# Raw weight halves kept in SBUF for their sums; joint accumulators read by ScalarE and added on GpSimd

## The chip, the cores and the metric

The kernel runs on one core of one Trainium2 chip. The metric is the device time of an execution in microseconds. Before the change the median of three runs is 1705.85 us (1702.62 to 1706.51). The profiled execution took 1705.2 us.

## The reference

Retention attention over 8 x 8 heads, then two two-layer networks on its rows; inputs are drawn as numpy arrays, the weights in float64.

```python
scores = (1 / sqrt(64)) * q @ k.T                      # 8 x 8 heads, 576 x 64
ret = scores * where(i >= j, gamma[h] ** (i - j), 0)   # decay by head
x = (ret @ v) -> 4608 x 512
h = x @ w_in           # 512 x 2048
g = h * sigmoid(1.702 * h)
x = g @ w_out          # 2048 x 512
h = x @ w_in2          # 512 x 2048
g = h - tanh(h)
out = g @ w_out2       # 4608 x 512
```

## The kernel before

Every product runs as three TensorE passes over a high and a low part of each operand (`PASS`), so each f32 tile is split before its use: a copy of the high part on ScalarE, a subtraction for the low part on VectorE. The 4608 rows form 9 blocks of 512; the 2048 hidden columns form 16 tiles (`NF`). A step is one block and one such tile.

The weights come as 64-bit patterns, in 64 chunks of 128 x 512, and are decoded on VectorE and ScalarE in thirds of a chunk (`dec_piece`); a step calls for one to three thirds. Decoded w_out and second-layer weights go to DRAM (`wd`), to be read again in each block.

The attention of a row tile is worked off in `attn_visit` at every second step, until all are done; GpSimd scales its inputs (`at_scale`). Blocks 0 and 1 of the first layer come in a part before the main loop. The main loop takes steps 32 to 143: blocks 2 to 8, sixteen steps each. A step issues the 12 matmuls of the first layer (`mm_in`, L616), perhaps an attention visit, the activation (`act_a`: tanh on ScalarE L630, the product on VectorE L632), the split of a tile for the second product (`split_direct`, ScalarE L728, VectorE L729), stores, and until step 82 four `outs` pieces, the second product (`mm_out`, L812). Blocks 2, 3 and 4 feed that product straight from SBUF; the others store g (`gd`) and load it later (`gl`, L723).

Some matrix products of blocks are formed by Strassen-like sums, which need fewer multiplications and sums of weights and of activations. Blocks 6 and 8 (`SUMMED`) form the activations' sums: `sums` (L1233 to L1236), five stores `gs` for each pair of steps (`stores`, L1206). The weights' sums are formed in two generators that are advanced one piece in each step of the main loop from step 48 on:

- `w2_prep` loads raw halves of w_in2 that the decoding had stored in DRAM (`wr`), splits them, forms sums on GpSimd (L960) and stores them (`wq`).
- `t_prep`, behind it, does so for w_out: loads of raw halves, 32 subtractions on VectorE (L995), 16 splits (ScalarE L990, VectorE L991), 16 stores `wt` (L981).

Both use the two tiles `spare` (four places, `room`), taken from the tag "y" at step 48.

Behind the main loop stand 16 steps of the second network's plain kind (`mm_std`, L1046), then 32 units of the paired kind (`mm_part` L1059, `copied`, `added` L1339, `act_2` L646 to L655). Between them `outs` hands out units of a second product. Of these, units 80 to 135 are joint: seven stages (`STAGES`) of eight units, with four accumulators in PSUM (`mm_joint`, L753). At a stage's end `evac_joint` empties them. Where nothing is to be added, ScalarE copies the accumulator into an "o" tile (L783); where a sum kept in DRAM is to be added, it was loaded by `kept_load` (L770, four loads at once, two units before the end), and VectorE reads accumulator and kept tile at once (L786). The result is stored on ScalarE's own DMA queue by `copies_out` (L824).

SP issues nearly all other DMAs, in program order: a DMA that waits for a semaphore holds those behind it. `w_ahead` issues the weight pairs (`wos`, L272; joint L286) and `g_ahead` the `gl` loads, both ahead of use; `wq_load` (L1027, L1036) loads the prepared sums of w_in2. The order of instructions on each engine is that of the code, which the helpers write by step numbers.

Of the kernel before, what the change touches and what calls it, by code (L numbers as in the profile page):

```python
# [54 lines left out]
def kernel(  # L55
# [45 lines left out]
    w2_d = {}  # L101
# [5 lines left out]
    part = {}  # L107

# [32 lines left out]
    def dec_b(m, f, c):  # L141
        hi, _, e, z = half[m, f, c]
        nc.vector.scalar_tensor_tensor(
            out=e, in0=hi, scalar=-(2 ** 31), in1=e, op0=ALU.bitwise_and, op1=ALU.bitwise_or
        )
        del stg[m, f, c]
        o = z.bitcast(F32)
        nc.vector.tensor_tensor(out=o, in0=z.bitcast(F32), in1=e.bitcast(F32), op=ALU.mult)
        half[m, f, c] = o
        if (m, c) == (1, 0):  # L150
            part[m, f, c] = half.pop((m, f, c))
        if (m, c) == (0, 1):
            part["raw", f, c] = o
# [8 lines left out]
    def dec_c(m, f, c):  # L162
# [6 lines left out]
        elif m == 0 and f % 5 < 3:  # L169
            sv = wos_p.tile([P, 2, DM], F32R, tag=f"wos{f % 5}", name="ws")  # L170
# [8 lines left out]
    def dec_d(m, f, c):  # L179
# [12 lines left out]
        if (m, c) == (0, 1):  # L192
            wos[f] = sv

    def dec_store():
        while part:
# [5 lines left out]
            if (m, c) == (1, 0):  # L202
                w2_d[f] = dram.tile([P, BLK], F32, tag=f"w{m}{f}{c}", name="wr")
                nc.sync.dma_start(out=w2_d[f], in_=sv)
                continue
# [4 lines left out]
    PAIRED = [q + i * NF // 2 for q in range(NF // 2) for i in range(2)]  # L210
    chunks = [(m, f, c) for m in range(2) for c in range(2) for f in (PAIRED if (m, c) == (1, 0) else range(NF))]
# [221 lines left out]
    def bat_x(b):  # L433
# [3 lines left out]
        if b % BPB == 0:  # L437
            xh[j], xl[j] = (
                x_p.tile([P, KD, BLK], F32R, tag="y" if j == 2 else "x", name=n, bufs=2 if j == 2 else 4)
# [149 lines left out]
    def step_of(o):  # L589
        v, f = divmod(o, NF)  # L590
        return ORDER[v] * NF + f if v < NB else o
# [81 lines left out]
    gs = {}  # L673
    n_items = n_steps + NJ
# [26 lines left out]
    def g_load(x):  # L701
# [6 lines left out]
        if spot == 0:  # L708
            gl[x] = t_p.tile([P, BLK], F32, tag="gl", name="gl", bufs=2)
# [48 lines left out]
    def kept_load(k):  # L758
# [3 lines left out]
        if name is None or q != NF // 2 - 3:  # L762
            return
        for y in range(4):
            r, m = divmod(y, 2)
            if y < 2:
                t = second["pool"].tile([P, BLK], F32, tag="o", name="kept", bufs=3)
            else:
                t = turn("t")
            nc.sync.dma_start(out=t, in_=kept_d[name, r, m])  # L770
            kept_t[y] = t

    def evac_joint(k, y):
# [4 lines left out]
        if base is None:  # L778
            if y < 3:
                o = second["pool"].tile([P, BLK], F32, tag="o", name="o", bufs=3)  # L780
            else:
                o = p_p.tile([P, BLK], F32, tag="p", name="o")
            nc.scalar.activation(out=o, in_=acc[y], func=ACTF.Copy, scale=0.5)  # L783
# [10 lines left out]
        copies.append((dst, o))  # L794
        copies_out(1)
# [67 lines left out]
    def g_ahead(x):  # L863

        while second and n_g[0] <= min(x + (7 if joint_item(x) else 4), n_b[0] + 3 + joint_item(x), n_items - 1):
# [14 lines left out]
    def out_units():  # L880

        for k in range(n_steps):
            w_ahead(k)
            if joint(k):
                kept_load(k)
                for y in range(4):
                    if y % 2 == 0:
                        g_ahead(N1 + 2 * (k - N1) + y // 2)
                    mm_joint(k, y)
# [6 lines left out]
            for m in range(4):  # L896
                mm_out(o, m)
# [10 lines left out]
    raw = {}  # L908
# [12 lines left out]
    def w2_prep():  # L921

        h = slice(0, DM // 2), slice(DM // 2, DM)
        waiting = []

        def store():
            while waiting:
                n, sv = waiting.pop()
                nc.sync.dma_start(
                    out=wq_d[q][:, n * 2 * DM:(n + 1) * 2 * DM], in_=sv.rearrange("p a n -> p (a n)").bitcast(F32)  # L930
                )

        def halves_of(n, src):
            sv = room[seen["room"] % 4]
            seen["room"] += 1
            kv = sv.rearrange("p a (k c) -> p (a k) c", c=2 * P).rearrange("p k (a c) -> p k a c", a=2)
            src = src.rearrange("p (k c) -> p k c", k=KD)
            nc.scalar.activation(out=kv[:, :, 0], in_=src, func=ACTF.Copy)
            nc.vector.tensor_tensor(out=kv[:, :, 1], in0=src, in1=kv[:, :, 0].bitcast(F32), op=ALU.subtract)
            waiting.append((n, sv))  # L940

        def load(q):
            raw[q] = [t_p.tile([P, DM], F32, tag="gl", name="wr", bufs=2) for _ in range(2)]
            for i in range(2):
                nc.sync.dma_start(out=raw[q][i], in_=w2_d[q + i * NF // 2])

        for q in range(NF // 2):
            while n_dec[0] < 3 * (2 * NF + 2 * q + 3):
                yield
            load(q)  # L950
            yield
            wq_d[q] = dram.tile([P, 8 * DM], F32, tag=f"wq{q}", name="wq")
            lo, hi = raw.pop(q)
            halves_of(0, lo)
            yield
            store()
            halves_of(2, hi)
            yield
            store()
            sub = lambda o, a, b: nc.gpsimd.tensor_tensor(out=o, in0=a, in1=b, op=ALU.subtract)  # L960
# [523 lines left out]
```

## Time and profile before

| | |
|---|---|
| median of three runs | 1705.85 us |
| the profiled execution | 1705.2 us, its span 1703.4 us |
| TensorE busy | 1651.0 us, 97% |
| VectorE, ScalarE, GpSimd busy | 1228.3, 886.6, 110.6 us |
| DMA | 510.60 MB, mean 300 GB/s |

The span is the time from the first to the last instruction that the profiler saw. PE is TensorE's matmuls, DVE VectorE, ACT ScalarE, POOL GpSimd, SP the engine that issues DMAs. PEclk is the granted share of TensorE's clock. An arrow in a wait points to what ended it. A DMA share of 1.00 means that all 16 transfer engines are busy.

### The profile page before, as it was taken

Reading aid. Unit: us, or ns where it says so; the run is one execution under the profiler, and the core shown is the slowest. Engines: PE = TensorE matmul, PEld = TensorE weight load, DVE = VectorE, ACT = ScalarE, POOL = GpSimd, SP = SyncE. Lnnn points to the kernel's source line nnn. Section 1 sums busy time; section 2 is a strip of 40 time slices with the busy share of each in tenths; the row PEclk is TensorE's granted clock in tenths of the full one; section 3 lists DMA queues with packets and bytes.
Section 4 is the critical chain, followed back from the end, with each engine's and each line's share of the span. In section 5 each row is a group of like instructions: output and inputs, shape, how many; then the busy total and the mean of one; then the engine's idle time right before and its main releaser. Section 6 shows DMA issues by size and latency. Waiting matters only on the chain.

```text
span 1703.4 us, 25300 instructions
## 1 busy us (share of the span) xinstructions
PE 1651.0 (97%) x8874; PEld 1342.8 (79%) x8874; DVE 1228.3 (72%) x1958; ACT 886.6 (52%) x1633; POOL 110.6 (6%) x99
## 2 busy tenths in 40 slices
PE   7999999999999998899999998999999999999999
PEld 4787888887888787688778777778888888888887
DVE  6787887778877866567678887777876777766632
ACT  5443433434433232456677666656665676656632
POOL 2101001212123100000000000000000000000000
PEclk9999999999999999999999999999999999999999
DMA  9666679888899989998899988989899988989962
GB/s 274 180 211 228 226 262 326 285 293 324 310 351 337 363 316 362 325 340 281 296 347 313 342 292 312 342 286 359 307 328 346 316 303 312 320 304 311 360 212 87
DMA packets 195503, 510.60 MB, mean 300 GB/s; under 512 B 21808, under 2 KB 31152, under 8 KB 186416
## 3 DMA queue, kind: packets, MB, share of 16 engines
q1 hardware_dynamic: 182704, 486.88, 82.2%
q10 hardware_dynamic: 12672, 22.11, 3.5%
q8 instruction: 70, 1.15, 0.3%
q14 instruction: 57, 0.47, 0.1%
HBM read 361.05 MB, written 147.85 MB: 299 GB/s over the span
## 4 chain that ended last, share of the span: by engine, by line
PE 75%; DMA 12%; DVE 8%; ACT 2%; issue 2%; SPq 1%; ACTq 0%; DVEq 0%
PE acc L816 23%; PE h L616 14%; PE acc L812 12%; PE x L1059 8%; PE acc L753 5%; PE y L1059 4%; PE h L1046 2%; PE w L1059 2%; DMA gs<-spare 2%; DMA gs<-t 1%; DMA gl<-gs 1%; DMA wos<-wd 1%; PE pat L538 1%; DMA gl<-gd 1%; DVE t L632 1%
## 5 line engine op out<-in xcount | busy, mean ns | idle before, releaser
L616 PE MATMUL h<-xh,wi 128*128 128x512 f32 x1152 | 372.3, 394 | 6.6 <-DVE t L632 5.8
L816 PE MATMUL acc<-wos,g 128*128 128x512 f32 x1344 | 329.6, 390 | 4.0 <-DVE kept L786 3.9
L816 PEld LDWEIGHTS acc<-wos,g 128*128 128x128 f32 x1344 | 252.4, 188 | 57.4 <-DVE kept L786 4.4
L728 ACT ACTIVATE g<-gl 128x512 fp32r<-128x512 f32 x222 | 139.3, 628 | 268.1 <-PE acc L816 173.2
L616 PEld LDWEIGHTS h<-xh,wi 128*128 128x128 f32 x1152 | 217.3, 189 | 56.3 <-DVE t L632 7.1
L729 DVE TENSOR_TENSOR g<-gl,g 128x512 fp32r<-128x512 f32 x222 | 152.1, 686 | 147.0 <-ACT g L728 146.4
L616 PE MATMUL h<-xl,wi 128*128 128x512 f32 x576 | 225.4, 391 | 0.4 <-DVE xl L445 0.4
L1059 PE MATMUL x<-xo,wq 128*128 128x512 f32 x768 | 195.1, 389 | 1.3 <-DVE h L1339 1.3
L812 PE MATMUL acc<-g,wos 128*128 128x512 f32 x768 | 189.0, 396 | 6.2 <-DMA wos<-wd 5.9
L812 PEld LDWEIGHTS acc<-g,wos 128*128 128x128 f32 x768 | 144.4, 190 | 39.2 <-issue 7.5
L1059 PEld LDWEIGHTS x<-xo,wq 128*128 128x128 f32 x768 | 144.0, 188 | 32.0 <-DVE h L1339 2.1
L131 ACT ACTIVATE e<-e,ebias 128x512 int32<-128x512 int32 x64 | 46.4, 724 | 208.1 <-DVE e L129 202.8
L632 DVE SCALAR_TENSOR_TENSOR t<-t,h 128x512 f32<-128x512 f32 x144 | 97.6, 682 | 54.4 <-ACT t L630 54.2
L653 DVE SCALAR_TENSOR_TENSOR pl<-pl,sq 128x512 f32<-128x512 f32 x144 | 99.5, 691 | 39.6 <-ACT pl L650 37.4
L630 ACT ACTIVATE t<-h 128x512 f32<-128x512 f32 x144 | 83.4, 587 | 85.1 <-PE h L616 59.9
L616 PEld LDWEIGHTS h<-xl,wi 128*128 128x128 f32 x576 | 108.7, 189 | 22.9 <-DVE xl L445 1.1
L655 DVE COPY_PREDICATED t<-marks,pl 128x512 f32<-128x512 int32 x144 | 109.4, 760 | 14.8
L753 PE MATMUL acc<-g,wos 128*128 128x512 f32 x408 | 104.9, 396 | 12.5 <-issue 3.7
L650 ACT ACTIVATE pl<-sq,abias 128x512 f32<-128x512 f32 x144 | 104.3, 724 | 4.7
L651 ACT ACTIVATE marks<-sq,sbias 128x512 f32<-128x512 f32 x144 | 102.0, 708 | 0.0
L753 PEld LDWEIGHTS acc<-g,wos 128*128 128x128 f32 x408 | 77.2, 191 | 31.2 <-issue 13.0
L1059 PE MATMUL y<-xo,wq 128*128 128x512 f32 x384 | 99.3, 395 | 0.0
(129 smaller groups left out, 2301.1 us busy)
## 6 DMA issues: line engine op xcount, KB each, us to landing
wos<-wd SPq DMA_DIRECT2D x176, 512.0 KB, 5.6
gd<-t SPq DMA_DIRECT2D x208, 256.0 KB, 5.2
gl<-gd SPq DMA_DIRECT2D x202, 256.0 KB, 5.3
wq<-wq SPq DMA_DIRECT2D x32, 1024.0 KB, 7.4
at<-in_attn_dram SPq DMA_DIRECT2D x29, 1024.0 KB, 6.6
stg<-in_w_dram SPq DMA_DIRECT2D x48, 512.0 KB, 6.7
wq<-wq SPq DMA_DIRECT2D x32, 768.0 KB, 8.9
wd<-ws SPq DMA_DIRECT2D x32, 512.0 KB, 5.4
```

Source lines behind the costliest of these rows:

```text
L616: nc.tensor.matmul(h, lhsT=win[f][:, a, k], rhs=xs[b][:, k], start=(n == 0), stop=(n == 3 * KD - 1))
L632: nc.vector.scalar_tensor_tensor(out=t, in0=t, scalar=1.0, in1=h, op0=ALU.add, op1=ALU.mult)
L650: nc.scalar.activation(out=pl, in_=sq, func=ACTF.Square, bias=abias)
L651: nc.scalar.activation(out=small, in_=sq, func=ACTF.Relu, bias=sbias, scale=-1.0)
L653: nc.vector.scalar_tensor_tensor(out=pl, in0=pl, scalar=CB, in1=sq, op0=ALU.add, op1=ALU.mult)
L655: nc.vector.copy_predicated(out=t, mask=small.bitcast(I32), data=pl)
L728: nc.scalar.activation(out=g[:, 0], in_=t, func=ACTF.Copy)
L729: nc.vector.tensor_tensor(out=g[:, 1], in0=t, in1=g[:, 0].bitcast(F32), op=ALU.subtract)
L753: nc.tensor.matmul(acc[y], lhsT=wo[:, a, m * P:(m + 1) * P], rhs=g[:, b], start=fresh and q == 0 and n == 0, stop=q == NF // 2 - 1 and n = ...
L812: nc.tensor.matmul(acc[m], lhsT=wh[:, m // 2, a, m % 2 * P:(m % 2 + 1) * P], rhs=g[:, b], start=first, stop=last)
L816: nc.tensor.matmul(acc[m], lhsT=g[:, a, c], rhs=wo[:, b], start=first, stop=last)
L1059: nc.tensor.matmul(ps, lhsT=wq[q][t][:, o // 2, o % 2 * 2 + k, a], rhs=xo[i][k][:, b], start=first and n == 0, stop=n == 5, skip_group_che ...
```

## The change

Three things change, and the order of pieces with them.

1. Raw w_out and w_in2 halves are decoded straight into one of three places in SBUF (`raw_place`). They belong to `room`, which now has five places: four in the `spare` tiles and one in a "gl" tile; the other two take the splits' results. Only the first three pairs of w_out still go through DRAM (`AWAY`). A pair that is complete joins a list `todo`, and each step advances the list by one or two pieces. If a place is wanted while its pair is still in `todo`, the list is advanced there and then. The chunks of w_out and the steps of block 2 follow the order of pairs (`PAIRED`); decoding goes at three thirds a step up to step 50, two up to step 82 and slower behind it.
2. `evac_joint` always reads the accumulator by ScalarE; a kept tile is added on GpSimd. The result goes out in `stores`, on SP. Kept tiles are loaded one by one, one unit before the end, all in "t" tiles.
3. `w_ahead` is called behind the first quarter of a unit in place of ahead of it; stores of the activations' sums come in another order, and two of their tiles come from `room`.

```diff
@@ raw_place, dec_b @@
+    def raw_place():
+        i = turn_of["raw"] % 3
+        turn_of["raw"] += 1
+        while users.get(i) in todo:
+            some_todo(1)
+        users[i] = "open"
+        return room[i].bitcast(F32), i
...
-        o = z.bitcast(F32)
+        i, q = divmod(f, NF // 2)
+        if m == c or m == 0 and q < AWAY:
+            o = z.bitcast(F32)
+        else:
+            if i == 0:
+                pairs_raw[m, q] = raw_place()
+            o = pairs_raw[m, q][0][:, i]
         nc.vector.tensor_tensor(out=o, in0=z.bitcast(F32), in1=e.bitcast(F32), op=ALU.mult)
@@ dec_d @@
+            i, q = divmod(f, NF // 2)
+            if i and q < AWAY:
+                late_t.append(q)
+                late_start()
+            elif i:
+                t, n = pairs_raw.pop((m, q))
+                raw_to(t_prep(q, t), n)
@@ g_load @@
-            gl[x] = t_p.tile([P, BLK], F32, tag="gl", name="gl", bufs=2)
+            gl[x] = room[4][:, gl_turn[0] % 2].bitcast(F32)
@@ kept_load @@
-        if name is None or q != NF // 2 - 3:
+        if name is None or q != NF // 2 - 2:
             return
...
+        if y == 0:
+            stores(0)
+        kept_t[y] = t = turn("t")
+        nc.sync.dma_start(out=t, in_=kept_d[(name, *divmod(y, 2))])
@@ evac_joint @@
+        nc.scalar.activation(out=o, in_=acc[y], func=ACTF.Copy, scale=0.5)
+        if base is not None:
+            t, o = o, kept_t.pop(y)
+            nc.gpsimd.tensor_tensor(out=o, in0=t, in1=o, op=ALU.add)
...
-            o = kept_t.pop(y)
-            nc.vector.scalar_tensor_tensor(out=o, in0=acc[y], scalar=0.5, in1=o, op0=ALU.mult, op1=ALU.add)
...
-        copies.append((dst, o))
-        copies_out(1)
+        done.append((dst, o))
@@ out_units @@
-            w_ahead(k)
             if joint(k):
-                kept_load(k)
                 for y in range(4):
                     if y % 2 == 0:
                         g_ahead(N1 + 2 * (k - N1) + y // 2)
+                    if y == 1:
+                        w_ahead(k)
+                    kept_load(k, y)
                     mm_joint(k, y)
@@ main loop @@
-            dec_piece(2 if j == 2 or (j < 5 and n % 2) else 1)
-        some(prep, 1)
+            dec_piece(2 if n < 3 * NF + BEHIND else int(n < PAUSE or j == 7))
+        if n == 6 * NF - 1:
+            some_todo(999)
+        elif n < PAUSE:
+            some_todo(1 if n < 3 * NF + BEHIND or n % 2 else 2)
+        else:
+            some_todo(1)
```

How instructions move is shown at three places. First VectorE in block 2, in a step before (L632 and L729 are the activation and the split, the rest decodes a chunk):

```order
L632 SCALAR_TENSOR_TENSOR t<-t,h 128x512
L729 TENSOR_TENSOR g<-t,g 128x512
L143 SCALAR_TENSOR_TENSOR e<-stg,e 128x512
L148 TENSOR_TENSOR z<-z,e 128x512
L185 TENSOR_TENSOR ws<-z,ws 128x2x256
L129 TENSOR_SCALAR e<-stg 128x512
L132 TENSOR_SCALAR z<-stg 128x512
L503 TENSOR_TENSOR p<-pat,mt_sb 128x512 x2
L137 SCALAR_TENSOR_TENSOR z<-stg,z 128x512
```

The same stretch of a step after (L690 and L789 are the activation and the split; L1026 and L986 are t_prep's subtractions and its split):

```order
L690 SCALAR_TENSOR_TENSOR t<-t,h 128x512
L789 TENSOR_TENSOR g<-t,g 128x512
L190 SCALAR_TENSOR_TENSOR e<-stg,e 128x512
L1026 TENSOR_TENSOR spare<-spare 128x256 x4
L986 TENSOR_TENSOR room<-spare,room 128x2x256
L986 TENSOR_TENSOR spare<-spare 128x2x256
L201 TENSOR_TENSOR spare<-z,e 128x512
L241 TENSOR_TENSOR ws<-spare,ws 128x2x256
L176 TENSOR_SCALAR e<-stg 128x512
L179 TENSOR_SCALAR z<-stg 128x512
L1026 TENSOR_TENSOR spare<-spare 128x256 x2
L561 TENSOR_TENSOR p<-pat,mt_sb 128x512 x2
```

Eight instructions of t_prep, from the steps 107 to 130 before, stand in one step of block 2.

Second, the end of a joint stage. Before, VectorE (L649 to L655 are a second-layer unit's activation, `kept<-acc` and `t<-acc` the evacuation):

```order
L729 TENSOR_TENSOR wos<-gl,wos 128x512
L786 SCALAR_TENSOR_TENSOR kept<-acc_9132,kept 128x512
L786 SCALAR_TENSOR_TENSOR kept<-acc_9136,kept 128x512
L649 TENSOR_TENSOR t<-h_9352,t 128x512
L653 SCALAR_TENSOR_TENSOR pl<-pl,sq 128x512
L654 SCALAR_TENSOR_TENSOR pl<-pl,h_9352 128x512
L655 COPY_PREDICATED t<-marks,pl 128x512
L729 TENSOR_TENSOR wos<-gl,wos 128x512
L786 SCALAR_TENSOR_TENSOR t<-acc_9145,t 128x512
L786 SCALAR_TENSOR_TENSOR t<-acc_9149,t 128x512
```

After, ScalarE at a stage's end (L704 to L709 are its part of such a unit, L788 copies of a split, L1356 a copy):

```order
L788 ACTIVATE wos<-room 128x512
L838 ACTIVATE o<-acc_8990 128x512
L838 ACTIVATE o<-acc_8995 128x512
L704 ACTIVATE t<-h_9207 128x512
L706 ACTIVATE sq<-h_9207 128x512
L708 ACTIVATE pl<-sq,abias 128x512
L709 ACTIVATE marks<-sq,sbias 128x512
L1356 ACTIVATE m_9336<-y 128x512
L788 ACTIVATE wos<-gl 128x512
L838 ACTIVATE o<-acc_9003 128x512
L838 ACTIVATE o<-acc_9007 128x512
```

The two pairs of evacuations keep their distance from each other, with a unit's activation between them, on the other engine; GpSimd has twenty adds L841 behind its scaling of the attention's inputs.

Third, SP in block 8. Before, stores of w_out's sums (`wt`) stand among the activations' (`gs`), with loads `a` for the next sums:

```order
L981 DMA wt<-spare 128x1024 x2
L659 DMA gd<-t 128x512
L1206 DMA gs<-a_6264 128x512
L1206 DMA gs<-t 128x512
L1206 DMA gs<-spare 128x512
L1221 DMA a_6363<-gd 128x512 x2
L981 DMA wt<-spare 128x1024
L1206 DMA gs<-spare 128x512
L1206 DMA gs<-t 128x512
L981 DMA wt<-spare 128x1024
```

After, in block 8:

```order
L1230 DMA gs<-spare 128x512
L1230 DMA gs<-t 128x512
L1230 DMA gs<-spare 128x512
L1230 DMA gs<-t 128x512
L1230 DMA gs<-spare 128x512
L1245 DMA a_6411<-gd 128x512 x2
L1047 DMA wq<-wq 128x1024 x2
```

The wt stores are gone from these rows, and the first wq load stands behind a group of five stores.

## Rows read from the trace of the kernel before

**Rows 1.** The page's first part: busy time, share and count of each engine.
```profile
PE 1651.0 (97%) x8874; PEld 1342.8 (79%) x8874; DVE 1228.3 (72%) x1958; ACT 886.6 (52%) x1633; POOL 110.6 (6%) x99
```
**Rows 2.** TensorE's waits from 400 us on: total, times, longest.
```profile
PE acc L812 <- DMA wos<-wd: 5.9, 1, 5.9
PE h L616 <- DVE t L632: 5.8, 2, 4.2
PE acc L753 <- DVE t L786: 4.8, 4, 2.9
PE acc L816 <- DVE kept L786: 3.9, 1, 3.9
PE acc L753 <- issue: 3.7, 1, 3.7
PE acc L753 <- DMA wos<-wd: 3.4, 1, 3.4
PE acc L753 <- DVE kept L786: 2.1, 2, 1.2
```
**Rows 3.** Windows: length, busy time of PE, PEld, DVE, ACT, POOL, PEclk, DMA share, GB/s.
```profile
1180.00:1460.00 280.00, 280.00 (x1237) 231.86 (x1236) 212.43 (x318) 186.67 (x325) 0.00 (x0) 1.00 0.91 318
660.00:720.00 60.00, 48.97 (x192) 39.15 (x191) 32.08 (x50) 18.30 (x32) 0.00 (x0) 0.89 0.95 341
697.90:704.70 6.80, 6.13 (x15) 4.80 (x16) 3.16 (x5) 4.13 (x7) 0.00 (x0) 0.50 1.03 406
840.00:1120.00 280.00, 259.47 (x1108) 209.53 (x1107) 222.39 (x341) 186.76 (x325) 0.00 (x0) 0.98 0.91 320
162.33:273.26 110.93, 110.93 (x710) 90.02 (x708) 87.86 (x155) 45.33 (x87) 12.20 (x9) 1.00 0.75 256
```
**Rows 4.** ScalarE's waits from 640 to 690 us.
```profile
ACT t L630 <- DMA gs<-t: 17.5, 3, 7.7
```
**Rows 5.** DMA issues of the execution: count, size, median us to landing.
```profile
wr<-z SPq DMA_DIRECT2D x32, 256.0 KB, 5.1
wr<-wr SPq DMA_DIRECT2D x32, 256.0 KB, 5.8
wt<-spare SPq DMA_DIRECT2D x16, 512.0 KB, 5.2
wq<-wq SPq DMA_DIRECT2D x16, 512.0 KB, 7.2
```
**Rows 6.** Line 981: ns min/median/max, first and last start.
```profile
L981 SPq DMA_DIRECT2D wt<-spare x16: 319/413/1156, 577.3 to 644.2; - x16
```
**Rows 7.** Timeline of SP: start, us, instruction.
```profile
686.71 2.21 SPq L1027 DMA_DIRECT2D wq<-wq  x4
689.02 1.26 SPq L272 DMA_DIRECT2D wos<-wd  x2
```
**Rows 8.** Lines 786 and 783: count, busy us, mean ns, idle before.
```profile
L786 DVE SCALAR_TENSOR_TENSOR t<-acc,t 128x512 f32<-128x512 f32 x10 | 6.4, 682 | 0.0
L783 ACT ACTIVATE o<-acc 128x512 f32<-128x512 f32 x8 | 4.3, 589 | 0.0
```
**Rows 9.** Timeline of VectorE at the stage end near 990 us.
```profile
990.82 1.28 DVE L786 SCALAR_TENSOR_TENSOR t<-acc,t 128x512 f32<-128x512 f32 x2
```
**Rows 10.** Timeline of VectorE, line 137, in block 2.
```profile
211.74 1.81 DVE L137 SCALAR_TENSOR_TENSOR z<-stg,z 128x512 f32<-128x512 uint32 x1
...
218.72 0.68 DVE L137 SCALAR_TENSOR_TENSOR z<-stg,z 128x512 f32<-128x512 uint32 x1
```
**Rows 11.** Timeline of GpSimd in the same stretch.
```profile
211.69 1.30 POOL L332 TENSOR_TENSOR at<-at,qt_sb 128x512 f32<-128x512 f32 x1 [22.00 <-DMA at<-in_attn_dram]
```
**Rows 12.** Lines 995 and 991: t_prep's work on VectorE.
```profile
L995 DVE TENSOR_TENSOR wr<-wr 128x256 f32<-128x256 f32 x32 | 13.5, 421 | 0.6
L991 DVE TENSOR_TENSOR spare<-wr,spare 128x512 fp32r<-128x512 f32 x16 | 11.0, 686 | 5.3 <-ACT spare L990 5.3
```
**Rows 13.** VectorE's waits from 162.33 to 273.26 us.
```profile
DVE sbd L555 <- ACT xh L548: 9.8, 3, 3.3
```

More of the change, by code (lines that the diff above doesn't have):

```diff
@@ L107, with some, raw_to, some_todo @@
     part = {}
+    AWAY = 3
+    PAIRED = [q + i * NF // 2 for q in range(NF // 2) for i in range(2)]
+    room = []
+    todo = []
+    pairs_raw = {}
+    users = {}
+    turn_of = {"raw": 0, "sv": 0}
+    def some(it, n):
+        for _ in range(n):
+            next(it, None)
+    def raw_place():
[3 more added lines that the diff above has]
+            some_todo(1)
+        assert users.get(i) != "open"
+        users[i] = "open"
+        return room[i].bitcast(F32), i
+    def raw_to(it, i):
+        users[i] = it
+        todo.append(it)
+    def some_todo(n):
+        while n and todo:
+            try:
+                next(todo[0])
+                n -= 1
+            except StopIteration:
+                todo.pop(0)
+    late_t = []
+    def late_start():
+        while room and late_t:
+            q = late_t.pop(0)
+            t, n = raw_place()
+            for i in range(2):
+                nc.sync.dma_start(out=t[:, i], in_=r_d[q + i * NF // 2])
+            raw_to(t_prep(q, t), n)
+    def sv_place():
+        turn_of["sv"] += 1
+        return room[3 + turn_of["sv"] % 2]
     def wload(m, f, c):
@@ L756, in mm_joint, with kept_load @@
             )
-    def kept_load(k):
+    def kept_load(k, y):
         stage, q = divmod(k - N1, NF // 2)
         name = STAGES[stage][3]
-        if name is None or q != NF // 2 - 3:
+        if name is None or q != NF // 2 - 2:
             return
[L764 to L771, printed above, removed]
+        if y == 0:
+            stores(0)
+        kept_t[y] = t = turn("t")
+        nc.sync.dma_start(out=t, in_=kept_d[(name, *divmod(y, 2))])
     def evac_joint(k, y):
@@ L863, in g_ahead @@
     def g_ahead(x):
[L865 removed]
+        while second and n_g[0] <= min(x + (7 if joint_item(x) else 4), n_b[0] + 3 + joint_item(n_g[0]), n_items - 1):
             g_load(n_g[0])
@@ L933, in halves_of @@
[L933 to L960, printed above, removed]
-            sub(hi[:, h[0]], hi[:, h[0]], lo[:, h[0]])
-            sub(hi[:, h[1]], hi[:, h[1]], hi[:, h[0]])
-            sub(lo[:, h[0]], hi[:, h[1]], lo[:, h[0]])
-            sub(lo[:, h[1]], lo[:, h[1]], hi[:, h[1]])
-            yield
-            halves_of(1, hi)
-            yield
-            store()
-            halves_of(3, lo)
-            yield
-            store()
-            yield
@@ L1215, in firsts_load @@
         if u % 3 == 2:
-            ts = [t_p.tile([P, BLK], F32, tag="z", name="a1", bufs=3) for _ in range(2)]
+            ts = [room[3].bitcast(F32)[:, i] for i in range(2)]
         else:
@@ L1301 @@
             wq_load(0, True)
-    some(prep, 99)
     stores(1)
+    assert not todo and n_dec[0] >= 3 * (len(chunks) + 2), n_dec
     for q in (1, 2):
```

170 lines of the change are left out of this document (87 added, 83 removed).

## The prediction

> **What bounds the kernel now.** I read the busy times first. TensorE is busy for 1651.0 us, 97% of the span of 1703.4 us [rows 1], and the change leaves the number of its matmuls as it was. So three things can move the time: gaps in TensorE's work that close, gaps that open, and stretches at the lower of its two clocks. Next I read the waits of TensorE after 400 us [rows 2]. They name the second half's gaps: 5.8 us for the first layer's activation (L632), 5.9 us for a weight pair (wos), 10.8 us in all (4.8 + 3.9 + 2.1) for VectorE's evacuation of a joint accumulator (L786), and beside these 3.7 us of "issue" and 3.4 us for another weight pair. Last I read windows, to see what a gap costs with what follows it [rows 3]. From 1180 to 1460 us TensorE is never idle and does 1237 matmuls in 280 us, 4.42 in a microsecond, 0.226 us each. From 660 to 720 us 265 would go in and 192 did: 73 x 0.226 = 16.5 us are lost, though its busy share shows only 11. The rest is the clock: the 6.8 us right behind the gap for wos ran at 0.50 (1.2 of 2.4 GHz) and took 15 matmuls where 30 go, 3.4 us lost after the gap itself. From 840 to 1120 us, the joint units, 1108 matmuls ran: 129 x 0.226 = 29 us lost.
>
> From 162 to 273 us, block 2 (the first of the main loop), TensorE is busy for the whole 110.93 us [rows 3]. So the change can take from two places, and it puts new work into a third that is full.
>
> **The end of the first layer, 660 to 720 us.** What ends the wait for L632 is two steps away: ScalarE's tanh (L630) waited 17.5 us for stores gs<-t [rows 4], because it writes into a tile that a store still reads. Those stores are late because the transfer engines are full: a share of 0.95 at 341 GB/s [rows 3]. The change takes transfers out from right before this stretch. Before, each raw half of w_out and w_in2 is stored (wr<-z, 32 x 0.26 MB) and loaded again for its sums (wr<-wr, 32 x 0.26 MB, 16 of them w_out's), and w_out's sums are stored (wt<-spare, 16 x 0.52 MB) [rows 5], at 577 to 644 us [rows 6]. Those 16 loads and 16 stores are 12.6 MB, at 341 GB/s 37 us of full transfer engines, in the 85 us before the stretch. After, 26 of the 32 raw stores and 26 of the 32 loads are gone, and the stores wt stand in block 2's steps, where the share is 0.75 [rows 3]. With 37 us of transfers out of the way, stores that are late by 6 us should be in time: the gap of 5.8 us and some 3.4 us at half speed behind it go, with what is lost in shorter waits beside them 10 us. The second gap, for wos, has another cause: SP issues four loads wq right ahead of that pair [rows 7], 0.52 MB each [rows 5], 2.1 MB or 6 us at 341 GB/s, and these stay; two gl loads of 0.26 MB are even put ahead of it. So I take the first gap alone. Bounds: 0, if the last block's own stores fill the queue again, and 16.5, if all goes. I take -10.
>
> **The joint units, 840 to 1120 us.** The sums that are added to a kept one are read on VectorE, 20 instructions of 0.68 us, ten of them into a "t" tile; the stages without a kept sum are read by ScalarE, 8 instructions of 0.59 us [rows 8], and no wait in [rows 2] names L783. The 0.68 us are not the wait of up to 4 us. That is VectorE's queue: at the stage end near 990 us two L786 start at 990.82 us [rows 9], behind a second-layer unit's four instructions and a split in the same queue, and TensorE can't begin the next sum in that bank before. After, ScalarE reads every accumulator into a tile of its own, and GpSimd adds the kept tile behind it, off TensorE's path. ScalarE has a queue as well, but it is busy for 186.76 of the 280 us, VectorE for 222.39 [rows 3]. What is late next is ScalarE's own string of four activations of a second-layer unit and a split's copy, near 0.6 us each. A gap half as long as the one for wos is taken to cost half as much behind it, 1.7 us at half speed, and two of these gaps are of that size (2.9 and 3.9 us): 10.8 + 3.4 = 14 us, of which I take 12. The other 15 us of the stretch's loss are weight pairs, "issue" and gaps too short for a row: the kept loads now come one by one instead of four at once ahead of gl loads, and 28 stores leave ScalarE's queue for SP's. I give that -4, so -16 in all. Bounds: -8 (half of the L786 gaps come back as waits for ScalarE) and -21 (all 14, and the 7.1 of "issue" and wos).
>
> There are new costs here. GpSimd's 20 adds can hold VectorE; a kept tile sits in a "t" tile until GpSimd has added and SP has stored it; and SP stands at that store until GpSimd is done, with loads of weights queued behind it. In the trace of before a VectorE instruction (L137) took 0.68 us alone and 1.81 us while GpSimd worked [rows 10, 11]: 1.1 us a time, twenty times 22 us if each add held VectorE to that degree and all of it lay on the path; nothing if VectorE's 58 idle us of the 280 hide it. I take +3, near the lower end, because an evacuation no longer stands in VectorE's queue. The Trainium skill, "GPSIMD Engine Reference", section "8. Key points", says that GpSimd shares its SBUF interfaces with VectorE, and names contention with VectorE instructions that read two SBUF inputs. The trace agrees, with 1.81 us against 0.68 us; by that rule alone the adds would be dear in the joint units, where most of VectorE's work is of that kind, and the fourth rival is what it would give.
>
> **Block 2, 162 to 273 us.** Here w_out's sums go: 32 subtractions (13.5 us) and 16 splits (11.0 us) [rows 12], with 16 copies on ScalarE, which has room. VectorE is busy for 87.86 of 110.93 us [rows 3], so 23.07 us are free and 24.5 come: at least +1.4, if every idle moment is filled. It won't be. Of the idle time 9.8 us are the attention's waits for a copy on ScalarE [rows 13], long enough (3.3 us) for another instruction to stand in them; the rest is spread over short waits between two steps of one unit, and a queue in order can't use those for certain. Then 24.5 - 9.8 = +14.7 us. I take the middle, +8. It would show as TensorE waiting for a split (L729, line 789 after) or for L632 (line 690 after).
>
> **Sum.** 1705.2 - 10 - 16 + 3 + 8 = 1690 us for a run like the profiled one. That run (1705.2 us) stands 0.65 us under the median of 1705.85; I leave the sum as it is. The 26 raw stores that go from the early blocks I cost at nothing: the share there is 0.75 and TensorE has no gap.
>
> **Rivals.** First, all opens: the gap for wos goes too, since the queue is drained (-16.5), the joint units give -21 with no new cost, and VectorE fills every gap (+1.4): 1705.2 - 36.1 = 1669 us. For it: 37 us of transfers gone; against it: the 2.1 MB right ahead of wos.
> Second, the transfers were hidden anyway: the last block's own stores fill the queue and the first gap stays (0), the joint units give -12, and block 2 costs the full 14.7: 1708 us. For it: the last store wt is issued at 644 us [rows 6], and behind 660 us the share is still 0.95; against it: the joint units run at 320 GB/s without a gap of that length for a store.
> Third, slower: VectorE becomes the bound in block 2. Its queue is in order, so subtractions ahead of a split delay the unit that TensorE is about to take. If all 24.5 us come on the path, in four gaps of some 6 us, each followed by 3.4 us lost at half speed, that is 24.5 + 13.6 = 38 us, and with the other terms 1705.2 - 26 + 3 + 38 = 1720 us. It decides once TensorE loses more than 23 us between 162 and 275 us. For it: 24.5 us into 23.07; against it: TensorE has no wait there now, so the splits run ahead of it.
> Fourth, GpSimd holds VectorE in the joint units for the whole 22 us, on the path: 1705.2 - 10 - 16 + 8 + 22 = 1709 us.
> Fifth, the change doesn't do what it says: the places in SBUF come free too late, the sums stay late, nothing moves: 1705 us. The order of instructions speaks against it.
>
> **Chances.** The forecast 0.56, with 1676 to 1700 us as its own range (block 2 between 1.4 and 14.7, the other two places 6 us either way); the first rival 0.20, the second 0.09, the third 0.08, the fourth 0.05, the fifth 0.02. The range for 8 in 10 reaches from just under the first rival to just over the fourth, 1667 to 1711 us. A measurement of this kernel can tell 0.2%, 3.4 us, from no change. Faster by more than that: 0.56 + 0.20 and a fifth of the second, 0.78. Within it: half of the second, half of the fourth, the fifth, 0.09. Slower: the third and what is left of the second and fourth, 0.13.
>
> **What would show it.** In the joint units TensorE's waits should name no VectorE evacuation, and the reads by ScalarE (line 838 after) should cost under 3 us in all. The tanh's wait for gs<-t should be under 3 us, 660 to 720 us should hold some 235 matmuls, and a wait for wos of about 6 us should stay. Between 162 and 273 us VectorE should be busy for over 95% of the time, and TensorE should show some 7 us of waits for lines 789 or 690. The forecast is wrong if block 2's losses exceed 23 us, if the gap for L632's successor between 660 and 690 us stays, or if VectorE's instructions beside a GpSimd add take over 1.5 us.

## The result, and the profile after

The changed kernel takes 1726.66 us (1720.52 to 1729.16, four runs) against 1706.18 us: a ratio of 1.0118, interval 1.0086 to 1.015. It is slower by 20 us where 16 us less were forecast. The profiled execution has a span of 1727.3 us, 23.9 more than before.

TensorE does the same 8874 matmuls. It is busy for 10.7 us longer, for the most part because more of them run at the lower of its two clocks (1.2 of 2.4 GHz): the mean granted clock is 0.986, against 0.990 before, and 0.014 of the span less 0.010 of the span before is an estimated 7 us:

```profile
PE 1661.7 (96%) x8874; PEld 1347.4 (78%) x8874; DVE 1227.7 (71%) x1938; ACT 895.9 (52%) x1653; POOL 141.0 (8%) x119
```

Where the time went is read best from the start of the same matmul in both traces. The table has the difference (after less before, us) that each stretch adds; the numbers are worked out from the starts in the two traces.

| stretch, to the start of | before, us | added | forecast |
|---|---|---|---|
| block 2's first second-layer product | 166.7 | +0.4 | 0 |
| step 56 (block 2 and the steps behind it) | 301.4 | +10.8 | +8 |
| step 76 (steps 56 to 75) | 428.4 | +3.6 | 0 |
| step 132 (steps 76 to 131) | 641.1 | -1.9 | 0 |
| end of the first layer | 728.7 | -3.4 | -10 |
| first joint unit | 836.2 | 0.0 | 0 |
| joint units and the first units behind | 1129.2 | +14.4 | -13 |
| the rest | 1688.2 | +0.2 | 0 |

Only the joint units went the other way from what was forecast. TensorE's waits of the changed kernel from 400 us on (total, times, longest) answer to [rows 2]:

```profile
PE acc L813 <- DMA wos<-wt: 11.0, 5, 3.3
PE acc L813 <- DMA wos<-wd: 7.4, 2, 5.3
PE acc L866 <- DMA wos<-wd: 6.7, 1, 6.7
PE x L1079 <- DVE h L1361: 6.4, 3, 3.1
PE x L1079 <- ACT u L1356: 3.5, 1, 3.5
PE acc L866 <- DVE g L789: 3.0, 1, 3.0
```

The 10.8 us for the evacuation (L786) are gone, as forecast, and so is the 5.8 us gap for the first layer's activation. In their place the joint units wait 18.4 us for weight pairs and 9.9 us for parts of second-layer units (h, u), which earlier came in time. The windows answer to [rows 3], with the same columns: block 2, the end of the first layer, the joint units, and two stretches around the end of the first layer.

```profile
162.80:284.50 121.70, 115.41 (x712) 91.14 (x710) 110.58 (x203) 53.05 (x102) 11.94 (x9) 0.99 0.83 281
671.00:731.00 60.00, 50.28 (x207) 40.70 (x206) 33.32 (x51) 20.21 (x36) 0.00 (x0) 0.91 0.96 351
845.70:1145.00 299.30, 268.59 (x1130) 215.43 (x1129) 227.28 (x325) 198.47 (x350) 30.64 (x20) 0.97 0.88 308
600.00:640.00 40.00, 40.00 (x299) 32.38 (x299) 16.18 (x28) 10.21 (x21) 0.59 (x1) 1.00 0.36 136
680.00:720.00 40.00, 30.28 (x119) 24.15 (x118) 19.44 (x30) 12.97 (x22) 0.00 (x0) 0.87 1.01 379
```

In block 2 VectorE went from 87.86 to 110.58 us, 91% of a stretch that is 10.8 us longer (over 95% were forecast). At the end of the first layer 207 matmuls ran in 60 us, not the 235 forecast. In the joint units no engine is full, so the loss is in the order of waiting. ScalarE at the end of the last joint stage (start, us, instruction, idle before) shows it:

```profile
1129.88 1.08 ACT L838 ACTIVATE o<-acc 128x512 f32<-128x512 f32 x2
1136.17 0.60 ACT L704 ACTIVATE t<-x 128x512 f32<-128x512 f32 x1 [5.21 <-issue]
```

The reads of the accumulators (L838) are quick. Then the next tanh (L704) stands for 5.2 us. The profile names nothing that ended this wait ("issue"), but the tanh began 0.07 us after a kept sum's store had landed (1136.10 us). The tanh writes a "t" tile, and all second-layer results and the four kept sums of a stage take turns in six of these. Between 850 and 1145 us the tanh's waits for a t tile are these, first after, then before:

```profile
ACT t L704 <- DMA gd<-t: 12.4, 4, 4.6
ACT t L704 <- DMA x<-t: 7.4, 2, 6.5
ACT t L704 <- issue: 5.2, 1, 5.2
```
```profile
ACT t L646 <- DMA gd<-t: 7.5, 3, 4.6
ACT t L646 <- DVE kept L786: 4.5, 2, 2.2
ACT t L646 <- DVE t L786: 2.8, 1, 2.8
```

`gd<-t` is the store of an earlier second-layer result, `x<-t` that of a kept sum: 25 us, where before the same tanh waited 7.5 us for stores and 7.3 us for VectorE's evacuations. Behind the tanh stand ScalarE's copies: TensorE's wait of 3.5 us for `u` (L1356) in the list above ended 3 us later.

### The profile page after: what moved, and what is told of

Same layout as the page of the kernel before. It is cut to its first block, busy times and chain, and to the rows that moved or that the text cites. A ratio compares the mean times of both kernels' runs of the same rounds, so it can differ in the third digit from the quotient of the medians.

```text
span 1727.3 us, 25296 instructions
## 1 busy us (share of the span) xinstructions
PE 1661.7 (96%) x8874; PEld 1347.4 (78%) x8874; DVE 1227.7 (71%) x1938; ACT 895.9 (52%) x1653; POOL 141.0 (8%) x119
## 4 chain that ended last, share of the span: by engine, by line
PE 68%; DMA 8%; DVE 6%; ACT 2%; issue 2%; SPq 1%; POOL 0%; POOLq 0%; ACTq 0%; DVEq 0%
PE acc L870 22%; PE h L674 12%; PE acc L866 10%; PE x L1079 9%; PE y L1079 4%; PE acc L813 4%; PE h L1066 2%; PE w L1079 2%; DMA gd<-t 1%; DMA gs<-spare 1%; DMA wos<-wt 1%; DVE g L789 1%; PE pat L596 1%; DMA wos<-wd 1%; PE sc L554 1%
## 5 line engine op out<-in xcount | busy, mean ns | idle before, releaser
L866 PEld LDWEIGHTS acc<-g,wos 128*128 128x128 f32 x768 | 145.5, 192 | 47.6 <-ACT g L788 9.5
L788 ACT ACTIVATE g<-gl 128x512 fp32r<-128x512 f32 x110 | 69.1, 628 | 141.8 <-PE acc L870 83.3
L690 DVE SCALAR_TENSOR_TENSOR t<-t,h 128x512 f32<-128x512 f32 x144 | 97.7, 683 | 61.9 <-ACT t L688 61.8
L788 ACT ACTIVATE g<-room 128x512 fp32r<-128x512 f32 x112 | 70.1, 628 | 132.5 <-PE acc L870 86.4
L789 DVE TENSOR_TENSOR g<-gl,g 128x512 fp32r<-128x512 f32 x110 | 77.7, 707 | 80.0 <-ACT g L788 79.5
L789 DVE TENSOR_TENSOR g<-room,g 128x512 fp32r<-128x512 f32 x112 | 78.1, 698 | 73.9 <-ACT g L788 73.6
L713 DVE COPY_PREDICATED t<-marks,pl 128x512 f32<-128x512 int32 x144 | 114.3, 794 | 15.5 <-ACT g L788 0.5
L707 DVE TENSOR_TENSOR t<-h,t 128x512 f32<-128x512 f32 x112 | 78.1, 697 | 38.8 <-ACT t L704 29.4
```

The lines of the kernel that those rows point to most:

```text
L690: nc.vector.scalar_tensor_tensor(out=t, in0=t, scalar=1.0, in1=h, op0=ALU.add, op1=ALU.mult)
L713: nc.vector.copy_predicated(out=t, mask=small.bitcast(I32), data=pl)
L788: nc.scalar.activation(out=g[:, 0], in_=t, func=ACTF.Copy)
L789: nc.vector.tensor_tensor(out=g[:, 1], in0=t, in1=g[:, 0].bitcast(F32), op=ALU.subtract)
L866: nc.tensor.matmul(acc[m], lhsT=wh[:, m // 2, a, m % 2 * P:(m % 2 + 1) * P], rhs=g[:, b], start=first, stop=last)
```

## The experiments

Of each run its median, its ratio with interval, and what its joint units added are given, the last as in the table, from the first joint unit's start to the last row (after: +14.6, before: 0). Ratios are to the kernel before, run beside each experiment; what is said to hold by the medians compares differences from the median of those runs. The kernels e3, e8, e10 and e11 have the same joint code and gave +2.9, +2.6, +3.1 and +1.2: differences under 2 us say nothing. The joint number comes from one execution alone. That execution was longer than the median in e4 (by 7.7 us) and e9 (4.8), and shorter in e6 (3.1), e13 (5.9), e16 (6.7) and e18 (3.4); there the medians have to bear it out. Two theories stood at first: W, that the weights' loads come late on SP since they are called behind the unit's first quarter; and T, that the kept sums hold t tiles. G, that GpSimd holds VectorE, joined them.

**One part undone, or done alone.** In e1 `w_ahead` stands ahead of the unit again:

```diff
         for k in range(n_steps):
+            w_ahead(k)
...
-                    if y == 1:
-                        w_ahead(k)
...
-                if m == 1:
-                    w_ahead(k)
```

> The changed kernel, with the weight pairs issued ahead of each unit again. Theory W (in the joint units the weight pairs stand on SP behind activation loads that wait for a free tile): TensorE's waits for wos in the joint units, 18.4 us in all after, fall under 6 us; about 1710 us. Rival T (the kept tiles sit in the three t tiles until GpSimd has added and SP has stored, and the tanh that needs one waits, 25 us on ScalarE): the waits for wos stay, about 1726 us. Block 2's loss of 11 us stays by both.

1722.0 us, ratio 1.0091 (1.0057 to 1.0126); joint +9.5. The waits for weight pairs fell as W says, but the tanh's waits for t tiles grew from 25 to 30 us and held TensorE elsewhere (its waits in e1, 840 to 1145 us), for ScalarE's reads too (L838), which stand in one queue with the tanh:

```profile
PE acc L813 <- ACT o L838: 7.3, 4, 3.3
PE x L1076 <- DVE h L1358: 6.2, 5, 3.9
PE acc L813 <- DMA wos<-wd: 3.7, 1, 3.7
PE x L1076 <- ACT u L1353: 3.4, 1, 3.4
```

The time is between W's 1710 and T's 1726 us. By the joint units W is a part of 5 us; by the medians it is 2 us, which the two intervals don't tell from nothing. In e2 the two functions of the evacuation are those of before, in e3 both edits are made:

```diff
-            t, o = o, kept_t.pop(y)
-            nc.gpsimd.tensor_tensor(out=o, in0=t, in1=o, op=ALU.add)
+            o = kept_t.pop(y)
+            nc.vector.scalar_tensor_tensor(out=o, in0=acc[y], scalar=0.5, in1=o, op0=ALU.mult, op1=ALU.add)
```

> The changed kernel, with the evacuation of the joint accumulators as before: VectorE reads accumulator and kept tile, kept tiles loaded four at once, stores on ScalarE's queue. Theory T: ScalarE's waits for t tiles in the joint units fall from 25 to about 7 us, the waits of TensorE for L786 come back at about 10 us; about 1715 us. Theory W: the waits for wos stay and L786's come on top; about 1730 us.

1718.15 us, 1.0073 (1.0045 to 1.0101); joint +1.7, with VectorE's evacuation (L846 in this kernel) in TensorE's waits again, 7.9 us in all.

> The changed kernel, with both the evacuation and the place of the weight loads as before: raw halves in SBUF alone. By both theories the joint units are what they were before, and what is left is block 2 (+11), the late w_in2 sums near 387 us (+4) and the end of the first layer (-3 to -8): about 1715 us. If the joint units stay slow, something else of the change (tiles, order of stores) slows them.

1716.58 us, 1.0069 (1.0043 to 1.0095); joint +2.9, as expected. So the evacuation is the larger part, and with the old one the weights' place costs nothing here. Done alone on the kernel before:

> The kernel before, with only the weight pairs' loads moved behind the first quarter of a unit. Theory W: TensorE's waits for wos in the joint units rise from 4 to about 18 us; about 1718 us. Theory T: nothing changes, 1706 us.

1708.07 us, 1.0025 (1.0005 to 1.0046); joint +6.8 in an execution that was the longest of ten, though through waits for L786 (13.7 us against 10.8) more than for wos (5.9 against 4.1): neither theory's detail.

> The kernel before, with only the evacuation of the joint accumulators changed: all read by ScalarE, kept tiles one by one in t tiles, GpSimd's add, stores on SP behind the others. Theory T (kept tiles hold up the tanh): ScalarE waits 20 to 30 us for t tiles in the joint units, TensorE's waits for L786 go and others of 15 us come; about 1712 us. Rival W (only the weights' loads made the joint units slow): about 1692 us, as the 10.8 us for L786 go.

1719.2 us, 1.0092 (1.0072 to 1.0113); joint +16.7. The new evacuation alone turns the kernel slow, with the tanh waiting 36 us for t tiles. TensorE's waits for VectorE's evacuation are gone, but 12.6 us of waits for ScalarE's (L778 in this kernel) stand in their place.

**Tile, GpSimd or ScalarE itself.** e6 is e1 with the sum written into ScalarE's copy (`out=o, in0=o, in1=kept_t.pop(y)`), e7 is e1 with `nc.vector` in place of `nc.gpsimd` for the add.

> The changed kernel with the weights' loads ahead of the units again (e1), and GpSimd's sum written into ScalarE's copy, so that a t tile is free after the add and not after the store. Theory T: ScalarE's waits for t tiles fall from 30 to under 12 us, and the joint units gain 5 us or more against e1: about 1716 us. Rival G (GpSimd's adds themselves hold VectorE): nothing changes, about 1722 us.

1716.96 us, 1.0068 (1.0051 to 1.0085); joint +2.5, 7 us better than e1, by the medians too. The tanh's waits fell to 16.8 us, not under the 12 us expected.

> The changed kernel with the weights' loads ahead of the units again (e1), and the kept sums added on VectorE, 0.69 us each, in place of GpSimd, from and into the same tiles. Rival G: VectorE's instructions are no longer stretched to 1.7 us, the joint units gain 5 us or more: about 1715 us. Theory T: the t tiles wait for their stores as before, and VectorE has 14 us more to do: 1722 to 1726 us.

1722.99 us, 1.01 (1.0077 to 1.0122); joint +5.1. The time is T's, but the joint units are 4 us better than in e1 (the rest of e7's profiled execution was 3 us slower), so G is not nothing.

e9 has no kept sums at all:

```diff
-                    kept_load(k, y)
...
-            t, o = o, kept_t.pop(y)
-            nc.gpsimd.tensor_tensor(out=o, in0=t, in1=o, op=ALU.add)
```

> The changed kernel with the weights' loads ahead of the units again (e1), and with the kept sums left out: neither loaded nor added, ScalarE's copy of the accumulator is stored as it is. What it shows is the evacuation by ScalarE without t tiles and GpSimd. Theories T and G: the waits of the tanh for t tiles fall under 10 us, and the joint units, 9 us longer in e1 than before, end up 5 to 12 us shorter than before; about 1703 us. Rival S (ScalarE's own queue makes its reads late): the waits of TensorE for ScalarE's read stay near 9 us; about 1720 us.

1696.89 us, 0.996 (0.9945 to 0.9975); joint -18.5. This bounds from above what ScalarE's reads are worth: e9 also leaves out the 20 loads of kept sums (5.2 MB), which the kernel before has. TensorE's waits between 840 and 1145 us:

```profile
PE acc L813 <- DMA wos<-wd: 4.0, 1, 4.0
PE x L1074 <- DVE h L1356: 1.3, 1, 1.3
PE acc L813 <- ACT o L838: 1.0, 1, 1.0
```

and the tanh waits for no t tile. So 9.5 + 18.5 = 28 us (26 by the medians) are the price in e1 of all that belongs to the kept sums: loads, tiles, adds, and stores that wait for the adds. What of the path takes them? e12 to e16 moved it about, e12 from e6 (with e11's first half), e13 to e15 from the kernel before, e16 from e1.

> The kernel of e11, with the joint units of e6 (ScalarE reads, GpSimd adds into ScalarE's copy), and a sum stored from GpSimd's own DMA queue right behind its add, the others from ScalarE's. If what is left of the tanh's waits in e6 (17 us) comes from gd stores that stand on SP behind sums not yet added, they fall under 10 us and the joint units take 5 to 10 us less than before: about 1697 us. Rival G (GpSimd holds VectorE): the joint units stay as in e6, 2 us over before: about 1706 us.

1719.81 us, 1.0097 (1.0083 to 1.0112); joint +7.0. The tanh still waited 16.2 us; the stores' queue was not it. Both forecasts were too low.

> The kernel before, with only the joint units changed: ScalarE reads every accumulator into an o or p tile; the kept tiles are loaded behind the evacuation, at most two at a time in t tiles (one of four ahead of it), GpSimd adds each into ScalarE's copy 2.5 units after its load was issued, and SP stores it. Theory T (t tiles held by kept sums at the stage's end make the tanh late): the tanh's waits at the stage ends go, and most of the 18 us that e9 showed come: 1686 to 1696 us. Rival G (GpSimd's adds stretch VectorE, wherever they stand): 1700 us or more.

1708.96 us, 1.003 (1.0017 to 1.0043); joint -0.3 in the profiled execution, which was the shortest of twelve. By the time rival G's forecast came true and T's did not. But the tanh still waited 25.3 us for t tiles (11.2 for stores, 14.1 for GpSimd's adds), so the tiles were held here too, and the run decides nothing between the two.

> As e13, with the 20 adds on VectorE (14 us in all) in place of GpSimd. Theory T: as e13 or up to 5 us later: 1688 to 1700 us. Rival G: faster than e13 by 5 us or more, as nothing stretches VectorE.

1718.26 us, 1.0088 (1.0073 to 1.0103); joint +14.3. Both forecasts failed, and G's was the other way round: with the adds on VectorE the kernel is slower. SP, which issues ahead of the engines, stood at the stores of sums not yet added (SP's waits in e14, 840 to 1145 us):

```profile
SPq L810 <- DVE o L806: 49.4, 18, 8.7
```

and loads and stores stood behind them, the t tiles' own stores too (the tanh waited 31.7 us for them). That VectorE's 20 more instructions have no part in it is not shown. Then load, add and store went to GpSimd and its queue:

```diff
-            nc.sync.dma_start(out=t, in_=kept_d[(base, *divmod(y, 2))])
+            nc.gpsimd.dma_start(out=t, in_=kept_d[(base, *divmod(y, 2))])
...
-            nc.sync.dma_start(out=dst, in_=o)
+            nc.gpsimd.dma_start(out=dst, in_=o)
```

> The kernel before, with ScalarE reading every joint accumulator, and load of the kept tile, add and store all on GpSimd and its own DMA queue, one tile after the other, 1.5 units apart. In e13 SP stood 24.5 us at stores of sums not yet added, in e14 49 us. Theory Q (the queue: what waits for GpSimd stands in SP's queue ahead of other loads and stores, and t tiles come free late): SP's wait goes, the tanh's waits in the joint units fall under 12 us, 1688 to 1697 us. Rival G (GpSimd's adds stretch VectorE): 1703 us or more.

1709.02 us, 1.0037 (1.0021 to 1.0053); joint +3.6: theory Q fell, and the time is in G's range. SP no longer waited for GpSimd, yet a t tile was now held until GpSimd, in order, came to its add (ScalarE's waits in e15, 825 to 1145 us):

```profile
ACT t L646 <- DMA gd<-t: 21.2, 5, 7.6
ACT t L646 <- POOL o L797: 15.5, 2, 12.1
```

> The same in the changed kernel with the weights' loads ahead of the units again (e1). Theory Q: the joint units are 10 us or more shorter than before where e1 was 9 us longer; what stays is block 2 and the rest of the first half (+8), about 1698 us. Rival G: 1712 us or more.

1720.07 us, 1.0108 (1.0083 to 1.0134), again in G's range; joint +2.5, but in the shortest execution of six, and by the medians the kernel is 2 us faster than e1, not 7. The tanh waited 24.3 us for GpSimd's adds. In all of these the kept tile lay in a t tile. In e17 and e18 it does not:

```diff
-        kept_t[y] = t = turn("t")
+        kept_t[y] = t = own[y // 2][:, y % 2]
...
-        s1, s2 = (st_p.tile([P, 2, BLK], F32, tag="stg", name="xs", bufs=3) for _ in range(2))
+        if not own:
+            own.extend(st_p.tile([P, 2, BLK], F32, tag="stg", name="xs", bufs=3) for _ in range(2))
+        s1, s2 = own
```

In e17 and e18 a kept tile falls on an xs tile that is still to be read, so one operand of the second layer is not the reference's; number and sizes of the instructions are what they would be. So they show what the tile costs, but not where a kernel could find room for four tiles of their own.

> The kernel before, with ScalarE reading every joint accumulator; the kept tiles lie in two tiles that the second layer's preparation uses a few times (xs), not in the six t tiles; GpSimd adds into ScalarE's copy and stores from its own queue. Neither t tiles nor SP wait for a kept sum. Theory T: the tanh's waits for t tiles in the joint units fall to 10 us or less, the joint units get 10 to 18 us shorter, 1686 to 1696 us. Rival G: 1703 us or more.

1698.44 us, 0.9969 (0.9956 to 0.9981); joint -8.4. That is 2 us over T's range and clear of G's. Against e5, which has the same reads with the kept sums in t tiles, it is 19 us less by the medians.

> The same in the changed kernel with the weights' loads ahead of the units again (e1): the changed kernel with the step mended that cost it most. Theory T: the joint units 10 to 18 us shorter than before, what is left of the first half +8: 1694 to 1702 us. Rival G: 1712 us or more.

1708.37 us, 1.0023 (1.0009 to 1.0037); joint -8.8, 18 us better than e1; by the medians 14. That is over T's range (up to 1702 us) and under G's (from 1712). In neither does the tanh wait for a store or an add at all. In e18 it waits for its input alone; that row, and TensorE's waits, are

```profile
ACT t L704 <- DVE h L1363: 0.5, 2, 0.3
```
```profile
PE acc L813 <- DMA wos<-wd: 5.3, 2, 3.6
PE x L1079 <- DVE h L1363: 3.3, 2, 1.8
PE acc L813 <- DVE g L789: 2.3, 3, 1.0
PE acc L813 <- DVE wos L789: 1.5, 2, 1.2
PE acc L813 <- ACT o L838: 0.9, 1, 0.9
```

GpSimd's 20 adds are all there. T holds: e18 and e12 share adds and store queue, and differ by 15.8 us in the joint units, 10 us by the medians, by where the kept tile lies (and by the call of `stores` that goes with a t tile; e12's first half is e11's). T's forecasts of the time were too low, though: what e18 lacks to e9, 10 us in the joint units and 12 us by the medians, is left for the loads, the adds and GpSimd's hold on VectorE; no run parts these.

**The first half.** e8 is e3 with two edits, which are shown; e10 is e3 without the 32 subtractions, e11 is e3 with w_out's raw halves through DRAM and its sums in steps 78 to 93:

```diff
-        sub = lambda o, a, b: nc.vector.tensor_tensor(out=o, in0=a, in1=b, op=ALU.subtract)
+        sub = lambda o, a, b: nc.gpsimd.tensor_tensor(out=o, in0=a, in1=b, op=ALU.subtract)
...
+    while n_w[0] <= DIRECT * NF + 3:
+        wo_load(n_w[0])
+        n_w[0] += 1
     for q in (1, 2):
         wq_load(q, True)
```

> The kernel of e3 (raw halves in SBUF alone) with two edits at places far apart. First, the 32 subtractions of w_out's sums on GpSimd in place of VectorE: if VectorE's load makes block 2 slow, its loss falls from 11 us to under 4 us; if the waits for the order of pairs or for places make it slow, it stays. Second, the weight pairs of units 50 and 51 issued ahead of the four wq loads at the end of the first layer: if those 2.1 MB are what wos waits for, the gap of 6.7 us falls to under 2 us, with 3.4 us at half speed; if it is the last block's stores ahead of all of these, it stays. Together about 1700 us against 1716.

1713.79 us, 1.0051 (1.0032 to 1.007). Block 2 still lost 9.0 us. And the gap for wos went, but others came in its place, and the end of the first layer took no less time than in e3 (-3.9 against -4.2 us). TensorE's waits in e8 from 660 to 730 us, and what stood ahead of them on VectorE and ScalarE (start, us, instruction, idle before):

```profile
PE acc L872 <- DVE g L789: 4.2, 1, 4.2
PE acc L872 <- ACT g L788: 2.6, 1, 2.6
```
```profile
690.70 0.69 DVE L1260 TENSOR_TENSOR spare<-spare,a 128x512 f32<-128x512 f32 x1 [3.39 <-DMA a<-gd]
708.69 0.63 ACT L788 ACTIVATE g<-gl 128x512 fp32r<-128x512 f32 x1 [16.78 <-DMA gl<-gd]
```

The wait of 4.2 us is for a split (L789) that stood in VectorE's queue behind a sum of activations, whose load `a` was late. The wait of 2.6 us is for a gl load that stood behind the wos pairs.

> The kernel of e3 (raw halves in SBUF alone) with the 32 subtractions of w_out's sums left out; the splits stay. Theory V (VectorE's load makes block 2 slow): 13.5 us less on VectorE, and block 2's loss falls from 10 to under 4 us; about 1709 us. Rival P (the splits, which go from ScalarE to VectorE and back in two queues in order, or the waits for places): the loss stays at 8 us or more; about 1715 us.

1712.05 us, 1.0051 (1.0032 to 1.0069). Block 2's loss fell from 10.7 to 5.7 us: half is the subtractions' time on VectorE, the other half stays with the splits, or with waits for places, which the run doesn't part (V and P in part).

> The kernel of e3 with all of w_out's raw halves through DRAM again and its sums in steps 78 to 93 (440 to 530 us), w_in2's raw halves in SBUF as in the changed kernel. If block 2 was slow by the work put there, its loss of 10 us goes (under 2 us left), and the gain of 8 us at the end of the first layer stays, since the transfers are still done before 600 us: about 1705 us. Rival: the loss moves along to the new steps: about 1714 us.

1713.26 us, 1.0062 (1.0046 to 1.0078). Block 2 lost nothing, but steps 76 to 131 lost 7.9 us where e3 gained 1.9: the rival, the loss moved along. There TensorE waited for the activation behind the same work on VectorE (its waits in e11, 480 to 540 us):

```profile
PE h L674 <- DVE t L690: 6.7, 5, 2.3
```

## Why the prediction was wrong, step by step

**The step that failed** is the new cost in the joint units: "a kept tile sits in a "t" tile until GpSimd has added and SP has stored it", "I take +3". The mechanism was named, but its size was not 3 us: 18 us went with the tiles' place, which e18 mends (e18 against e1; 14 by the medians), and 28 us with all that belongs to the kept sums, the loads included (e9 against e1). The +3 came from idle time of VectorE, but the tiles' turn binds ScalarE's tanh. Four of six t tiles are kept sums at a stage's end where before it were two, each released only by a store behind an add; the prediction never counted them. The joint units came out at +14.4 us and not at -13: that is 27 of the 39 us between the forecast and the profiled execution. One of the prediction's own signs of being wrong showed too: an instruction of VectorE beside a GpSimd add took over 1.5 us (1.72 us, below).

**ScalarE's reads**: -16 was forecast. e9, without kept sums and their loads, has -18.5, with 1.0 us of waits for L838, and e18, with them, -8.8; so the reads' own share lies at or under 18.5 us and is open. As soon as the tanh waits for a tile, the reads behind it are late too: 12.6 us of waits for them in e5, against the 10.8 us for L786 that they replace. The prediction saw such a string on ScalarE, but not the wait inside it.

**The weights' loads** got no term of their own, and moving them brought no gain that a run shows. After, with them moved, the joint units took 5.1 us more than in e1 (2 by the medians), and in e4 the move alone cost 4 us by the medians.

**GpSimd's hold on VectorE** is real, but was not the fourth rival's 22 us. The predicate copies took 759 ns before, 867 ns in the changed kernel and 762 ns in e9 (VectorE, 825 to 1145 us; the first row is before, the next after, the third e9):

```profile
L655 DVE COPY_PREDICATED t<-marks,pl 128x512 f32<-128x512 int32 x47 | 35.7, 759 | 4.8
```
```profile
L713 DVE COPY_PREDICATED t<-marks,pl 128x512 f32<-128x512 int32 x44 | 38.2, 867 | 4.9 <-ACT g L788 0.5
```
```profile
L713 DVE COPY_PREDICATED t<-marks,pl 128x512 f32<-128x512 int32 x49 | 37.3, 762 | 5.0
```

The Trainium skill, "GPSIMD Engine Reference", section "8. Key points", names contention with VectorE instructions that have two SBUF inputs, as these copies do (marks and pl). The trace agrees: one such copy during a run of three adds took 1.72 us (first GpSimd, then VectorE):

```profile
1129.60 4.71 POOL L841 TENSOR_TENSOR t<-o,t 128x512 f32<-128x512 f32 x3 [1.80 <-ACT o L838]
```
```profile
1129.79 1.72 DVE L713 COPY_PREDICATED t<-marks,pl 128x512 f32<-128x512 int32 x1
```

Yet it is worth no more than the 10 to 12 us of the path by which e18 falls short of e9. Adds on VectorE gave the same time in e1's place (e7), and a longer one where SP's stores stood behind them (e14).

**Block 2**: +8 forecast, +10.8 measured, with TensorE waiting for the split (L789 and its copy L788), as said (its waits after, 160 to 300 us):

```profile
PE acc L866 <- DVE g L789: 5.0, 6, 1.9
PE acc L866 <- ACT g L788: 1.8, 1, 1.8
```

That VectorE's load is the cause is half shown: 5.0 us by e10. Moving the subtractions to GpSimd did not help (e8).

**The end of the first layer**: the gap for L632 went, 7.7 us up to the first matmul of L1066, near the 10 forecast. But 4.3 us came back behind it, as the wait for wos grew from 5.9 to 6.7 us and one of 3.0 us for g joined it. The transfers did get out of the way, as said: from 600 to 640 us the share is 0.36, against 0.84 before. But the stretch behind it is as full as it was: from 680 to 720 us the share is 1.01, and 17 stores of activations' sums and 13 loads of weights go out there (15.2 MB in all), as many as in the like 40 us before (670 to 710 us, 14.9 MB). They are what the second gap waits behind; the prediction had named the last block's stores, as the reason for its bound of 0. e8 fits this: loads in another order only moved the gaps.

**Steps 56 to 76** cost 3.6 us that no step had, at one gap of 2 us with 3.4 us at a granted clock of 0.50 behind it: w_in2's sums on GpSimd fell beside an attention visit, and VectorE's decoding there was slow (a mask of 0.42 us took 1.05 us). It is seen in the trace only; no run leaves this work out.

The third rival had the right sign and a time (1720 us) near the result, but by luck: block 2 was its mechanism, and block 2 lost 10.8 us, not 38.

## What to carry to other kernels

An instruction moved to a free engine was cheap here only where the tile that it reads and writes was free as well: count, at the fullest moment, how many tiles of a rotation the moved work holds, until when, and which engine takes the next one. A store that waits for a slower engine holds what stands behind it in its queue (in e14 SP stood 49.4 us at such stores). And leave the new work out once (e9): it bounds what the other half of an edit can be worth.

## What was not expected of the hardware

GpSimd's adds of 128x512 from SBUF took 1.55 us each (20 in 30.6 us). They held VectorE's instructions up to 1.72 us, and still the same adds on VectorE made the kernel no faster (e7, e14).

```profile
L841 POOL TENSOR_TENSOR t<-o,t 128x512 f32<-128x512 f32 x20 | 30.6, 1550 | 503.1 <-DVE t L707 364.8 <-ACT o L838 66.3 <-DMA room<-gs 37.0
```

Work taken from a full transfer queue shortened only the wait next behind it: after 12.6 MB less in front, the end of the first layer had a share of 0.96 at 351 GB/s, as full as before (0.95 at 341).
